# A recurrent attention followed by a SoLU block: first loads split and spread over two queues, one gate block turned on TensorE, one output half moved

## The chip, the cores and the metric

The kernel runs on one core of a Trainium2 chip. The metric is the device time of one execution in microseconds (us), measured without the profiler; the median over the runs counts. One execution was also profiled, and all views below come from that one. TensorE is called PE, VectorE DVE, ScalarE ACT, GpSimd POOL, SyncE SP.

## The reference

Two parts follow each other. The first is a gated linear recurrence over 4 batches, 8 heads, 768 time steps and a head dimension of 48; the second is a feed-forward block on the 3072 tokens, with 384 inputs, 1024 hidden values and 384 outputs.

```python
for t in range(S):
    state = alpha[:, :, t, :, None] * state + np.einsum('bhd,bhe->bhde', k[:, :, t], v[:, :, t])
    y[:, :, t] = np.einsum('bhd,bhde->bhe', q[:, :, t], state)
x = np.ascontiguousarray(y.transpose(0, 2, 1, 3)).reshape(B * S, H * D)
h = x @ w_in
e = np.exp(h - np.max(h, axis=-1, keepdims=True))
solu = h * e / (np.sum(e, axis=-1, keepdims=True) + 1e-09)
mu, var = mean and variance of solu over its last axis
out = ((solu - mu) / np.sqrt(var + 1e-06) * g_ln) @ w_out
```

Inputs q, k, v and alpha are float32. The two weight matrices arrive as float64, so the kernel reads them as pairs of 32-bit words and makes float32 of them itself.

## The kernel before, in words

**Tiling.** Time is cut into 6 groups of 128 steps; one group holds all 4 batches, so it is 512 tokens. Channels are handled transposed (channels on partitions, time along the free axis): the first 32 channels of a head form one block, the last 16 of two heads together another, 12 blocks in all in the tiles `aT` (alpha), `kT`, `qv`, `qe` and `hT`. Products of alpha over time come from scans on DVE: `scan_back` runs backwards over a third of the blocks into `hT`, `scan_on` forwards in `aT`. Keys are multiplied by the one, queries by the other; then `scores` (PE), `masked` (DVE), `read_state` and `read_values` (PE) give the attention output `x`, and `next_state` carries the state on.

**Turning.** The inputs of group 0, and k and q of group 1, are loaded with time on partitions (`load_first`) and turned on PE: `turned` multiplies 48 slices of 32 channels by the identity. The last 16 channels of the heads are first gathered by ACT into a contiguous tile (`ends_of`). All others, alpha of group 1 among them, are loaded in another layout (`load`) and turned by DVE's 32x32 transposes (`alpha_T`, lines L184 and L187). `alpha_over` is a range check of alpha: two passes on ACT over the loaded tile `an` (L201), which must run before the next alpha overwrites it.

**Weights.** Each matrix comes in four pieces of two blocks each, `fetch(i, slot, n)` loading n pieces beginning at piece i. A w_in piece takes 16 DMA issues, 8 of 32 rows and 8 of 16 rows (L505). `in_range` checks a piece on ACT (L522, L523), `bits` makes float32 in five DVE operations (L535 to L547), and `scaled` multiplies a w_out piece by the gain on ACT (L554).

**Feed-forward.** For a group g, `up(g, f)` makes hidden block f of 8: three matmuls into `h` (L366), exponential on ACT (L380), product with h on DVE (L381), square on ACT (L382). `down(n, half)` multiplies four of the eight blocks of one batch-and-group chunk n by w_out into a PSUM tile (L448); after both halves `finish(n)` applies the norm (DVE L457 to L466, POOL L470, ACT L472) and stores.

**Order.** The order on every engine is the order in which the program writes its instructions; each engine runs its own in that order. DMA issues take their turn in the queue of SP (nearly all) or ACT (constants). A start section handles the attention of group 0. Then a loop over f makes the hidden blocks of group 0, with `bits`, `in_range`, loads and `ends_of` for group 1 put between them by hand. Then comes a section, also by hand, that mixes the downs of group 0 with the attention of group 1:

```python
    bits(6)
    tk = three("tp_k", [(ps_a, "a2"), (ps_a, "a3"), (ps_h, "h")])
    turned(kn, ends_k, tk)
    load(k, kn, 2)
    array_sums(0, 1)
    down(0, 0)
    scaled(6)
    bits(7)
    token_sums(0)
    alpha_T(1)
    down(1, 0)
```

It ends with `read_values(1)`, `next_state(1)` and `finish(3)`. From there a loop over g = 1..6 and steps s = 0..7 runs `up(g, s)`, the attention of group g + 1 by a plan, and one half down of group g - 1 at each step, taken from the list `todo`, which is empty for g = 1.

Of the kernel before, what the change touches and what calls it, by code (L numbers as in the profile page):

```python
# [11 lines left out]
U32 = mybir.dt.uint32  # L12
# [4 lines left out]
P = 128  # L17
# [15 lines left out]
def fast_path(ctx, tc, q, k, v, alpha, moe_w_in, moe_w_out, moe_g_ln, out):  # L33
# [12 lines left out]
    nc = tc.nc  # L46
    B, H, S, D = q.shape
# [81 lines left out]
    def load(src, dst, g):  # L129
        t = slice(g * P, (g + 1) * P)  # L130
        for b in range(B):
            nc.sync.dma_start(
                out=dst[32 * b : 32 * b + 32].rearrange("t h u d -> t h (u d)"),
                in_=src[b, :, t, :].rearrange("h (t u) d -> t h (u d)", u=TQ),
            )
# [5 lines left out]
    def load_first(src, dst, g):  # L141
        t = slice(g * P, (g + 1) * P)
        for b in range(0, B, 2):
            nc.sync.dma_start(  # L144
                out=by_token(dst)[:, b : b + 2].rearrange("p b h d -> p (b h) d"),
                in_=src[b : b + 2, :, t].rearrange("b h p d -> p (b h) d"),
            )

    def ends_of(src, tag=None):

        ends = ring.tile([P, T4], FP, name=tag) if tag else two.tile([P, T4], FP, tag="two", name="ends")
        ends = ends.rearrange("p (b d) -> p b d", b=B)
        nc.scalar.copy(out=ends.rearrange("p b (h d) -> p b h d", h=H), in_=by_token(src)[:, :, :, E0:D])
        return ends

    def turned(src, ends, out, blocks=range(NB)):

        x = by_token(src)
        for j in blocks:
            for b in range(B):  # L160
                cols = x[:, b, j, 0:E0] if j < H else ends[:, b, E0 * (j - H) : E0 * (j - H) + E0]
                nc.tensor.matmul(
                    out[j // NP][32 * b : 32 * b + 32, j % NP], lhsT=cols, rhs=ident, start=True, stop=True,
                    tile_position=(0, 32 * b), skip_group_check=True,
                )
# [31 lines left out]
    def alpha_over(g):  # L197
        x = an.rearrange("p h u d -> p (h u d)")
        sq = one.tile([P, 768], FP, name="sq").bitcast(U8)[:, 0 : x.shape[1]]
        for i, sign in enumerate((1.0, -1.0)):  # L200
            nc.scalar.activation(  # L201
                out=sq, in_=x, func=AF.Relu, scale=sign, bias=mone, accum_out=over[:, g, i : i + 1]
            )
# [31 lines left out]
    def apart():  # L235
        for i in range(2):
            nc.scalar.mul(
                out=qv[:, H : 2 * H].rearrange("p (j i) t -> p j i t", i=2)[:, :, i], in_=qe, mul=parity[:, i : i + 1]
            )
# [22 lines left out]
    def scores(g, half, a=None):  # L262
        a = a or banks("a", [NP, P])
        for i in range(NP):
            h = half * NP + i
            for kb, qb in ((h, h), (H + h // 2, H + h)):
                for b in range(B):
                    nc.tensor.matmul(  # L268
                        a[b][:, i], lhsT=kT[quarter(b), kb], rhs=qv[quarter(b), qb], start=kb == h, stop=kb != h,
                        tile_position=(32 * b, 0), skip_group_check=True,  # L270
                    )
        masks[half] = a
# [141 lines left out]
    def warm(n, ps=ps_o, tag="o"):  # L414
        t = ps.tile([P, 512], FP, tag=tag, name="warm")
        for i in range(n):
            nc.tensor.matmul(t[:, 0:P], lhsT=ones, rhs=ones, start=True, stop=True)
# [71 lines left out]

    raws = {}  # L490

    def fetch(i, slot, n=1):

        kind, f = pieces[i]
        w = n * F // (2 if kind else KC)
        raw = room[:, 1536 * slot : 1536 * (slot + n)].bitcast(U32).rearrange("p (c f w) -> p c f w", f=w, w=2)
        if kind:
            parts = [(slice(0, P), c, moe_w_out[(f + c) * P : (f + c + 1) * P, :]) for c in range(2)]
        else:
            rows = moe_w_in[:, f * P : f * P + w].rearrange("(h d) f -> h d f", d=D)  # L500
            parts = [(slice(E0 * r, E0 * r + E0), c, rows[NP * c + r, 0:E0]) for c in range(2) for r in range(NP)]
            parts += [(slice(E1 * h, E1 * h + E1), 2, rows[h, E0:D]) for h in range(H)]
        for rows, c, src in parts:
            if float64:
                nc.sync.dma_start(out=raw[rows, c].rearrange("p f w -> p (f w)"), in_=src.bitcast(U32))  # L505
            else:
                dst = w_out[rows, f + c, 0:DM] if kind else w_in[rows, c, f * P : f * P + w]
                nc.sync.dma_start(out=dst, in_=src)
        for m in range(n):
            raws[i + m] = raw[:, :, w // n * m : w // n * (m + 1)]  # L510

# [37 lines left out]
    def scaled(i):  # L549

        f = pieces[i][1]
        for c in range(f, f + 2):
            w = w_out[:, c, 0:DM]
            nc.scalar.mul(out=w, in_=w, mul=g_col[:, c : c + 1])  # L554
# [27 lines left out]
    def inline(x, name):  # L582
        return nc.inline_tensor(np.ascontiguousarray(x, np.float32), name=name).ap()

    load_first(alpha, an, 0)
    nc.scalar.dma_start(out=ident, in_=inline(np.eye(P), "ident_c"))
    nc.scalar.dma_start(out=mask, in_=inline(np.triu(np.ones((P, P))), "mask_c"))
    odd = np.arange(P) // E1 % 2
# [10 lines left out]
        nc.gpsimd.memset(s, 0.0)  # L599
    nc.gpsimd.memset(state, 0.0)  # L600
    load_v_first(0)
    fetch(0, 3, 2)
    fetch(2, 1, 2)
    nc.vector.memset(ones, 1.0)
    nc.vector.memset(small_ones, 1.0 / 32)
# [5 lines left out]
        return [pool.tile([P, NP, P], FP, tag=tag, name=f"{name}{i}") for i, (pool, tag) in enumerate(where)]  # L611


    warm(18)
    t = three("tp_a", [(ps_a, "a0"), (ps_a, "a1"), (ps_a, "a2")])
    turned(an, ends_of(an), t)
    for i in range(3):
        nc.scalar.copy(out=aT[:, NP * i : NP * i + NP, 1:SW], in_=t[i])  # L618
        scan_back(0, i)
    t = three("tp_k", [(ps_a, "a3"), (ps_h, "h"), (ps_h, "h")])  # L620
    turned(kn, ends_of(kn), t)
    alpha_over(0)
    scan_on(0, 2)
    for i in range(3):
        part = slice(NP * i, NP * i + NP)
# [1 line left out]
    scan_on(0, 0)  # L627
    t = three("tp_q", [(ps_o, "o"), (ps_o, "o"), (ps_a, "a0")])
    turned(qn, ends_of(qn), t)
    for i in (2, 0, 1):  # L630
        if i == 1:
            scan_on(0, i)
        part = slice(NP * i, NP * i + NP)
        nc.vector.tensor_tensor(
            out=qe if i == 2 else qv[:, part], in0=t[i], in1=aT[:, part, 1:SW], op=ALU.mult
        )
        if i == 2:
            apart()
    scores(0, 0)
    t = [x.tile([P, NP, P], FP, tag=n, name="a_" + n) for x, n in ((ps_h, "h"), (ps_o, "o")) for _ in range(2)]  # L640
    scores(0, 1, t)
# [11 lines left out]
    for f in range(FC):  # L653
        p = 2 + f // 2
        up_mm(0, f)
        if f == 4:
            array_sums(0, 0)
        up_act(0, f)
        bits(p, f % 2)
        if f == 0:  # L660
            next_state(0)
            fetch(4, 3)
            load_first(k, kn, 1)
            load_first(q, qn, 1)
            load(alpha, an, 1)
        elif f == 1:
            in_range(2)
        elif f == 2:
            ends_k = ends_of(kn, "e")
        elif f == 3:  # L670
            in_range(3)
            ends_q = ends_of(qn, "u2")
        elif f == 4:
            fetch(5, 1)
            fetch(6, 2)
        elif f == 5:
            in_range(4)
            fetch(7, 3)
            load_v(1)
        elif f == 6:  # L680
            scaled(4)
        elif f == 7:
            scaled(5)
    bits(6)
    tk = three("tp_k", [(ps_a, "a2"), (ps_a, "a3"), (ps_h, "h")])
    turned(kn, ends_k, tk)
    load(k, kn, 2)
# [2 lines left out]
    scaled(6)  # L690
    bits(7)
    token_sums(0)
    alpha_T(1)
    down(1, 0)
    scaled(7)
    tq = three("tp_q", [(ps_a, "a0"), (ps_a, "a1")])
# [37 lines left out]
    read_begin()  # L734
    read_state(0)
    read_state(1)
    down(3, 1)
    read_state(2)
    read_state(3)
    alpha_over(2)  # L740
# [2 lines left out]
        scan_back(2, i)  # L743
    read_values(1)
    next_state(1)
    finish(3)

# [67 lines left out]
            next_state(a)  # L817

    centres = {4: (0, 1), 6: (2, 3), 7: (4, 5, 6, 7)}
    todo = []  # L820
    for g in range(1, G + 1):
        rise, att = g < G, g + 1 < G
        plan = {1: first, 2: second}.get(g, usual)

        def at(where, s):
            for what in plan[where].get(s, "").split() if att else ():
                attend(g + 1, what)

        after = None
        for s in range(FC):  # L830
            at("head", s)
            if rise:
                up(g, s)
            if after is not None:
                finish(after)
                after = None
            if s == 0 and g > 1:
                token_sums(g - 1)
            at("behind", s)
            for f in centres.get(s, ()) if g == 1 else ():  # L840
                centre(f)
            if rise and s:
                running(g, s)
            at("middle", s)
            if todo:
                n, half = todo.pop(0)
                down(n, half)
                if half:
                    after = n
            at("tail", s)  # L850
        if after is not None:
            finish(after)
        todo = [(n, half) for n in range(g * B, g * B + B) for half in range(2)]
# [476 lines left out]
```

## Time and profile before

| | before |
|---|---|
| median of 3 runs (lowest to highest) | 408.06 us (406.02 to 409.49) |
| the profiled execution: its own time | 412.59 us |
| its span from first to last instruction | 409.5 us |
| mean granted PE clock | 0.981 |
| busy: PE, DVE, ACT, POOL | 378.3, 249.8, 146.8, 118.2 us |
| moved by DMA | 30.82 MB |

PE is busy for 92% of the span. Busy shares are averages over stages with different limits, so they have to be read stage by stage: PE is idle for 31 us in all, and all but a few of these lie in the first 165 us and behind the last matmul. A matmul in float32 shows as two records in the trace.

### The profile page before, as it was taken

What the parts mean: (1) busy time and instruction counts of PE and PEld (TensorE: products, weight loads), DVE (VectorE), ACT (ScalarE), POOL (GpSimd) and SP (SyncE); (2) the same over time, 40 slices, a digit from 0 to 9 for tenths busy, and PEclk for the clock granted to TensorE, in tenths of its full rate; (3) what the DMA queues carried; (4) which work ended last, traced back from release to release, by engine and by line L of the source; (5) the groups of instructions that cost most, each with busy time, mean ns of one, the idle gap of its engine ahead of it and who ended that gap; (6) DMA issues with size and microseconds to landing.
All of it is one profiled execution on the core that took longest, in us unless ns stands there. A gap on an engine that the chain in (4) does not pass through costs nothing.

```text
span 409.5 us, 11054 instructions
## 1 busy us (share of the span) xinstructions
PE 378.3 (92%) x4897; PEld 229.9 (56%) x4897; DVE 249.8 (61%) x412; ACT 146.8 (36%) x253; POOL 118.2 (29%) x121
## 2 busy tenths in 40 slices
PE   8786999888997798999999999999999999999991
PEld 8673435456663457555657555666556575554550
DVE  1968789994939884698691894665864322322201
ACT  3533675653332625223443143342251222222110
POOL 4010000030005794075620446210474211333110
PEclk9996999998999999999999999999999999999997
DMA  9966969403329303633030931004200000000110
GB/s 189 183 159 175 216 189 195 106 19 76 81 64 151 78 3 82 78 98 75 23 99 11 162 76 47 9 15 73 26 19 21 22 3 21 19 21 19 40 38 29
DMA packets 86409, 30.82 MB, mean 75 GB/s; under 512 B 67912, under 2 KB 84560, under 8 KB 86352
## 3 DMA queue, kind: packets, MB, share of 16 engines
q1 hardware_dynamic: 85904, 29.89, 33.6%
q8 instruction: 40, 0.66, 0.7%
q10 hardware_dynamic: 448, 0.14, 0.1%
q14 instruction: 17, 0.14, 0.1%
HBM read 25.30 MB, written 4.72 MB: 73 GB/s over the span
## 4 chain that ended last, share of the span: by engine, by line
PE 61%; DVE 21%; SPq 6%; ACT 5%; issue 4%; DMA 2%; DVEq 0%; ACTq 0%
PE o L448 23%; PE h L366 20%; PE y L300 9%; PE a L268 4%; SPq L505 3%; PE kv L342 3%; DVE room L381 3%; DVE aT L209 2%; SPq L144 2%; DVE sT L279 2%; DVE p L392 2%; DVE top L538 1%; DVE aT L184 1%; DMA qn<-in_q_dram 1%; DVE low L546 1%
## 5 line engine op out<-in xcount | busy, mean ns | idle before, releaser
L366 PE MATMUL h<-x,w_in 128*128 128x512 f32 x288 | 135.0, 610 | 8.1 <-DVE g_col L559 4.6
L448 PE MATMUL o<-w_out,room 128*128 128x385 f32 x384 | 133.0, 491 | 1.1 <-DVE least L223 1.1
L448 PEld LDWEIGHTS o<-w_out,room 128*128 128x128 f32 x384 | 71.6, 190 | 57.2 <-issue 15.2
L366 PEld LDWEIGHTS h<-x,w_in 128*128 128x128 f32 x288 | 53.5, 193 | 68.5 <-issue 50.7
L470 POOL TENSOR_TENSOR r<-sums,mhalf 128x1 f32<-128x1 f32 x24 | 13.2, 549 | 192.2 <-DVE sums L462 192.1
L381 DVE TENSOR_TENSOR room<-h,e 128x512 f32<-128x512 f32 x40 | 27.5, 687 | 58.9 <-ACT e L380 58.8
L380 ACT ACTIVATE e<-h 128x512 f32<-128x512 f32 x40 | 23.9, 596 | 83.3 <-PE h L366 83.3
L392 POOL TENSOR_TENSOR p<-p,e 128x512 f32<-128x512 f32 x30 | 42.5, 1417 | 22.7 <-ACT e L380 22.5
L382 ACT ACTIVATE u<-room 128x512 f32<-128x512 f32 x40 | 25.2, 630 | 50.3 <-DVE room L381 50.3
L279 DVE TENSOR_TENSOR sT<-a,mask 128x512 f32<-128x512 f32 x44 | 27.3, 680 | 12.3 <-PE a L268 12.3
L268 PE MATMUL a<-qv,kT 32*128 32x128 f32 x704 | 26.3, 292 | 5.0 <-DVE qv L721 2.0
L268 PEld LDWEIGHTS a<-qv,kT 32*128 32x128 f32 x704 | 23.4, 198 | 12.1 <-issue 2.9
L392 DVE TENSOR_TENSOR p<-p,u 128x512 f32<-128x512 f32 x30 | 23.9, 797 | 9.8 <-ACT u L382 9.8
L209 DVE TENSOR_TENSOR_SCAN hT<-aT,unit 128x516 f32<-128x516 f32 x18 | 21.8, 1256 | 8.2 <-ACT aT L618 8.1
L472 ACT ACTIVATE o_sb<-o,r 128x384 f32<-128x384 f32 x20 | 11.6, 580 | 40.2 <-POOL r L470 37.0
L209 DVE TENSOR_TENSOR_SCAN aT<-aT,seed 128x516 f32<-128x516 f32 x18 | 25.0, 1387 | 0.6
L300 PE MATMUL y<-sT,vn 128*32 128x128 f32 x768 | 23.0, 274 | 1.2 <-issue 0.7
L351 DVE TENSOR_TENSOR state<-state,kv 128x512 f32<-128x512 f32 x10 | 6.9, 688 | 28.2 <-PE kv L342 28.2
L233 POOL TENSOR_TENSOR kT<-kT,hT 128x1024 f32<-128x1024 f32 (+1 forms) x8 | 13.7, 1736 | 31.8 <-DVE kT L184 31.8
L300 PEld LDWEIGHTS y<-sT,vn 128*32 128x32 f32 x768 | 20.8, 110 | 3.6 <-issue 2.6
L331 ACT COPY x<-y 128x384 f32<-128x384 f32 x24 | 11.5, 479 | 31.6 <-PE y L300 31.6
L300 PE MATMUL y<-qv,state 32*32 32x128 f32 x1280 | 20.2, 278 | 2.0 <-issue 1.6
(129 smaller groups left out, 385.4 us busy)
## 6 DMA issues: line engine op xcount, KB each, us to landing
out_dram<-o_sb SPq DMA_DIRECT2D x24, 192.0 KB, 1.9
an<-in_alpha_dram SPq DMA_DIRECT2D x20, 192.0 KB, 4.1
room<-in_moe_w_out_dram SPq DMA_DIRECT2D x8, 384.0 KB, 3.8
kn<-in_k_dram SPq DMA_DIRECT2D x16, 192.0 KB, 4.2
qn<-in_q_dram SPq DMA_DIRECT2D x16, 192.0 KB, 3.5
vn<-in_v_dram SPq DMA_DIRECT2D x5, 512.0 KB, 5.7
room<-in_moe_w_in_dram SPq DMA_DIRECT2D x16, 128.0 KB, 3.6
kn<-in_k_dram SPq DMA_DIRECT2D x4, 384.0 KB, 5.8
```

The lines of the kernel that those rows point to most:

```text
L209: nc.vector.tensor_tensor_scan(out=o, data0=a, data1=s, initial=1.0, op0=ALU.mult, op1=ALU.add)
L233: nc.gpsimd.tensor_tensor(out=kT[:, part], in0=kT[:, part], in1=hk[:, part], op=ALU.mult)
L268: nc.tensor.matmul(a[b][:, i], lhsT=kT[quarter(b), kb], rhs=qv[quarter(b), qb], start=kb == h, stop=kb != h, tile_position=(32 * b, 0), sk ...
L279: nc.vector.tensor_tensor(out=sT[:, b, half * NP : half * NP + NP], in0=a[b], in1=mask[:, None, :].to_broadcast([P, NP, P]), op=ALU.mult,)
L300: nc.tensor.matmul(y_bank(b)[quarter(r), a], lhsT=lhsT, rhs=rhs, start=(b, r) not in begun, stop=stop, tile_position=(row, 32 * r), skip_g ...
L366: nc.tensor.matmul(h, lhsT=w_in[:, a, f * P : (f + 1) * P], rhs=d["x"][:, a].rearrange("p b t -> p (b t)"), start=(a == 0), stop=(a == KC ...
L380: nc.scalar.activation(out=e, in_=h, func=AF.Exp)
L381: nc.vector.tensor_tensor(out=u, in0=h, in1=e, op=ALU.mult)
L382: nc.scalar.activation(out=u2, in_=u, func=AF.Square)
L392: eng.tensor_tensor(out=p, in0=d[0][i] if f == 1 else p, in1=d[f][i], op=ALU.add)
L448: nc.tensor.matmul(d["o"][:, 0 : DM + 1], lhsT=u_of(g, f)[:, b * P : b * P + P], rhs=w_out[:, f], start=(f == 0), stop=(f == FC - 1), skip ...
L470: nc.gpsimd.tensor_tensor(out=r, in0=s[:, 3:4], in1=mhalf, op=ALU.pow)
```

## The change

- Alpha of group 0 is fetched by `load_halves` in eight issues (first four heads of each batch, then the other four) instead of two, and turned in two steps: heads first, each third copied out by ACT as soon as it is there, the gathered ends last. A copy of one column is put first on ACT. The warm-up matmuls go from 18 to 11.
- w_in piece 0 is fetched alone. Piece 1 is fetched by the ACT queue, in three portions of 4, 5 and 7 issues between ACT's work of the start section. `fetch` gets arguments for the queue and for the portion.
- `alpha_over(0)` moves from the start section to f = 2 of the loop over group 0's hidden blocks. The load of group 1's alpha goes behind it, now with time on partitions.
- Group 1's alpha is turned on PE ahead of group 1's k, with `ends_of` at f = 6 and three ACT copies; `alpha_T(1)` goes.
- `down(3, 1)` and `finish(3)` move from the hand-written section into the loop: the half down to step 1 of g = 1, its finish to step 2.

```diff
+    def load_halves(src, dst, g):
+        t = slice(g * P, (g + 1) * P)
+        for h in range(0, H, NP):
+            for b in range(B):
+                nc.sync.dma_start(
+                    out=by_token(dst)[:, b, h : h + NP], in_=src[b, h : h + NP, t].rearrange("h p d -> p h d")
+                )
...
-    def fetch(i, slot, n=1):
+    def fetch(i, slot, n=1, queue=nc.sync, some=slice(None)):
...
-        for rows, c, src in parts:
+        for rows, c, src in parts[some]:
             if float64:
-                nc.sync.dma_start(out=raw[rows, c].rearrange("p f w -> p (f w)"), in_=src.bitcast(U32))
+                queue.dma_start(out=raw[rows, c].rearrange("p f w -> p (f w)"), in_=src.bitcast(U32))
...
-    load_first(alpha, an, 0)
+    load_halves(alpha, an, 0)
...
-    fetch(0, 3, 2)
+    fetch(0, 3)
     fetch(2, 1, 2)
...
-    warm(18)
+    nc.scalar.copy(out=mean_sb[:, 0:1], in_=ones[:, 0:1])
+    warm(11)
     t = three("tp_a", [(ps_a, "a0"), (ps_a, "a1"), (ps_a, "a2")])
-    turned(an, ends_of(an), t)
+
+    def evict_a(i):
+        nc.scalar.copy(out=aT[:, NP * i : NP * i + NP, 1:SW], in_=t[i])
+
+    turned(an, None, t, range(H))
+    evict_a(0)
+    ends = ends_of(an)
+    evict_a(1)
+    turned(an, ends, t, range(H, NB))
+    evict_a(2)
     for i in range(3):
-        nc.scalar.copy(out=aT[:, NP * i : NP * i + NP, 1:SW], in_=t[i])
         scan_back(0, i)
     t = three("tp_k", [(ps_a, "a3"), (ps_h, "h"), (ps_h, "h")])
     turned(kn, ends_of(kn), t)
-    alpha_over(0)
+    fetch(1, 4, queue=nc.scalar, some=slice(0, 4))
     scan_on(0, 2)
...
     turned(qn, ends_of(qn), t)
+    fetch(1, 4, queue=nc.scalar, some=slice(4, 9))
     for i in (2, 0, 1):
...
         if i == 2:
             apart()
+    fetch(1, 4, queue=nc.scalar, some=slice(9, 16))
     scores(0, 0)
...
             load_first(q, qn, 1)
-            load(alpha, an, 1)
         elif f == 1:
             in_range(2)
         elif f == 2:
+            alpha_over(0)
+            load_first(alpha, an, 1)
             ends_k = ends_of(kn, "e")
...
         elif f == 6:
             scaled(4)
+            ends_a = ends_of(an, "e")
         elif f == 7:
             scaled(5)
     bits(6)
+    t = three("tp_a1", [(ps_a, "a2"), (ps_a, "a3"), (ps_o, "o")])
+    nc.gpsimd.memset(aT[:, :, 0:1], 0.0)
+    turned(an, ends_a, t)
+    for i in range(3):
+        evict_a(i)
     tk = three("tp_k", [(ps_a, "a2"), (ps_a, "a3"), (ps_h, "h")])
     turned(kn, ends_k, tk)
...
     token_sums(0)
-    alpha_T(1)
     down(1, 0)
...
     read_state(1)
-    down(3, 1)
     read_state(2)
...
     next_state(1)
-    finish(3)
...
-    todo = []
+    todo = [None, (3, 1)]
...
-            if todo:
-                n, half = todo.pop(0)
+            step = todo.pop(0) if todo else None
+            if step:
+                n, half = step
                 down(n, half)
                 if half:
                     after = n
```

## The prediction, made before the changed kernel ran

> **What bounds the kernel now.** I read the table of busy time by stretch first, to find where TensorE (PE) is not the bound. Columns: start:end, length, then busy us and instructions of PE, PE weight loads, VectorE (DVE), ScalarE (ACT), GpSimd (POOL); the granted PE clock; DMA share; GB/s.
>
> ```profile
> 0.00:20.00 20.00, 16.04 (x352) 14.77 (x356) 10.68 (x23) 9.27 (x13) 5.11 (x12) 1.00 1.04 183
> 20.00:40.00 20.00, 14.69 (x303) 10.25 (x303) 14.87 (x21) 7.86 (x16) 1.83 (x3) 0.83 0.63 162
> 60.00:80.00 20.00, 19.02 (x253) 10.66 (x251) 18.16 (x25) 11.65 (x23) 0.00 (x0) 1.00 0.80 159
> 80.00:100.00 20.00, 15.68 (x135) 10.52 (x134) 16.56 (x31) 10.14 (x19) 4.22 (x5) 0.91 0.07 21
> 120.00:140.00 20.00, 16.03 (x46) 7.12 (x44) 17.93 (x23) 7.24 (x13) 9.77 (x7) 1.00 0.54 91
> 220.00:260.00 40.00, 40.00 (x346) 23.13 (x336) 26.23 (x46) 12.21 (x21) 17.81 (x16) 1.00 0.38 75
> ```
>
> From about 160 us on PE is never idle; whatever the change gains or loses, it does so before. The first 20 us are DMA (share 1.04); 20 to 95 us is a chain through DVE, fed by ACT. So I read the timeline of that part next (start, length, engine, line; in brackets the idle time before it and its releaser).
>
> ```profile
> 20.25 1.77 POOL L180 COPY vn<-room 128x1024 f32<-128x1024 f32 x2 [14.56 <-DMA room<-in_v_dram]
> 29.39 0.95 DVE L535 TENSOR_SCALAR top<-room 128x768 uint32<-128x768 uint32 x1 [3.24 <-DMA room<-in_moe_w_in_dram]
> 34.06 5.33 PE L366 MATMUL h<-x,w_in 128*128 128x512 f32 x6 [4.55 <-DVE g_col L559]
> 49.20 0.63 ACT L382 ACTIVATE sT<-room 128x512 f32<-128x512 f32 x1 [0.76 <-DVE room L381]
> 50.06 0.96 DVE L538 SCALAR_TENSOR_TENSOR top<-room,top 128x768 uint32<-128x768 uint32 x1
> 50.25 0.59 ACT L380 ACTIVATE sT<-h 128x512 f32<-128x512 f32 x1
> 50.94 0.68 DVE L381 TENSOR_TENSOR room<-h,sT 128x512 f32<-128x512 f32 x1
> 67.22 1.12 ACT L554 ACTIVATE w_out<-w_out,g_col 128x384 f32<-128x384 f32 x2 [1.84 <-DVE w_out L547]
> 86.66 0.69 DVE L713 TENSOR_TENSOR qe<-tp_q,aT 128x512 f32<-128x512 f32 x1
> 93.84 3.62 PE L268 MATMUL a<-qv,kT 32*128 32x128 f32 x62 [2.02 <-DVE qv L721]
> 100.18 2.07 PE L268 MATMUL a<-qv,kT 32*128 32x128 f32 x64
> 106.80 2.86 PE L448 MATMUL o<-w_out,room 128*128 128x385 f32 x8
> 133.02 2.84 PE L366 MATMUL h<-x,w_in 128*128 128x512 f32 x6 [2.68 <-DVE room L381]
> ```
>
> To be seen: v lands at 20.25. DVE waits 3.24 us for the first two w_in blocks, which land together at 29.2. PE idles 4.55 us and comes back slow: the first up takes 5.33 us where one at full clock takes 2.84. At 50.9 the product of block 3 waits for its exponential and its own engine almost equally. At 93.84 sixty-two score matmuls take 3.62 us after a pause, sixty-four later ones 2.07.
>
> **Start.** The chain from here on begins when w_in block 0 has landed, since DVE is ready at 26.15. Alone the block is 0.79 MB instead of 1.57, which looks like a gain. But in the built program each DMA signals one of eight semaphores in turn, and an issue waits until the transfer that used its semaphore last has landed. Read off the waits of the built instructions: before, the eighth w_in issue is the one that waits for v to land; now, with eight alpha issues instead of two and the ACT issues taking their turns, it is the third issue of block 0. The seventh alpha issue also waits for the mask, and k for the parity constant, which (issue at 1.64, 3.3 us to landing) arrives at 4.9; k was issued at 2.62. Alpha's own tail and all behind it slip by up to 2.3 us; I take 1.0, as SP runs ahead of the transfers. Nine of the sixteen block-1 issues, now on ACT, go out before v has landed: 0.56 MB, which at the 183 GB/s of the first row takes 3.0 us of a full DMA stretch. From v's landing the remaining fourteen issues of block 0 follow each other every 0.46 us (SP issued 16 in 7.38 us), the last lands 2.2 us after its issue, and some wait in turn for block-1 issues on ACT that hang on the same semaphores: about 8.8 us in all. With v at its old 20.2 that is 29.0 (−0.2); with 2.3 + 3.0 us more it is 34.3 (+5.1). Since block 1's packets are larger and partly fill holes I take a little under the middle: **+2.0**. The earlier alpha scans, the activation table loaded ahead, and seven fewer warm-up matmuls end before that landing and cost or bring nothing while DVE waits there; without that cover k's and q's delay would show, about 1 us.
>
> [...]
>
> **Overflow check moved.** `alpha_over(0)`, two passes over alpha, sat at 11.0 to 14.4 us on ACT, free time before q came. It now stands after the square of up block 2 (49.20) and before `ends_k` and the exponential of block 3 (50.25). Its twin for group 1 ran from 95.43 to 98.78: 3.35 us. DVE was ready for block 3's product at 51.02, the exponential ended at 50.84, so nearly all of it goes into DVE's chain. Later DVE gaps (before 55.23, 61.14, 64.02) are waits for ACT behind the same chain and move along. **+3.35**; between 0 (if ACT had slack) and 3.35. The alpha load of group 1 behind it on SP is late too, but is needed only some 12 us later; `fetch(5,1)` queued behind that load lands with about 3 us to spare. `ends_a` (0.6 us) goes in before the exponential of block 7, which DVE waits for (0.72 us idle before 64.02): **+0.6** (0 to 0.6).
>
> **Alpha of group 1 turned by PE.** Gone from DVE: transposes from 76.16 to 79.00, 2.84 us. Added on PE: 48 turns, 2.84 us by the k turns of 61.77 to 64.61. Added on ACT: three copies of 0.6. Those copies stand behind `scaled(5)`, which waits for DVE's block 5 until 67.22 and ends at 68.34. The k turns reuse the first two banks, so PE cannot start them before 68.94, where it started them at 61.77. Behind them in PE's queue, with their rows of before: k turns and sums 4.64, down(0,0) 2.79, rows 0.59, down(1,0) 2.79, q turns 1.95, mean 1.63, down(0,1) 2.79, mean 0.91, last q turns 1.08. That ends at 88.11, and the product `qe` at 86.66 needs it: **+1.5**. DVE's scans alone would begin 0.9 us earlier than before, so −0.9 is the lower end. PE idles over 4 us ahead of 68.94, as long as the 4.55 us after which it came back slow; I price the slow time by the scores, 3.62 against 2.07: **+1.6** (0, as after the 2.68 us pause before 133.02, to 2.5, as in 5.33 against 2.84). With PE late, the pause before the scores at 93.84 disappears and they run in 2.07: **−1.55** (0 if a pause stays).
>
> **Down(3,1) moved.** From 97.4 to 118.5 PE is full, so taking out eight matmuls brings up(1,0) forward by **−2.8**. They land behind up(1,1), ahead of the 2.68 us in which PE waits for DVE before 133.02, so they cost little there. `finish(3)` goes with them: its four DVE operations (119.19 to 120.26, then idle time) now stand in DVE's full stretch before `scan_on(2,1)`: **+1.1**.
>
> **Sum.** 2.0 + 3.35 + 0.6 + 1.5 + 1.6 − 1.55 − 2.8 + 1.1 = **+5.8 us**. The profiled execution took 412.59 us (span 409.5 and 3.1 around it), so it would take 418.4, 1.4% more; the median of the runs is 408.06, so I predict **413.8 us**. All lower ends give −4.35 (403.7), all upper ends +11.4 (419.5).
>
> **Rivals.** A, not slower: block 0 is there when DVE is, at 26.2. The 3.24 us gap goes, PE pauses 1.3 us instead of 4.55 and the first up takes 2.84: −5.7 instead of +2.0, in all −1.9, **406.2 us**. It decides once block 0 lands before about 28 us, and with a smaller term elsewhere it is clearly faster. For it: half the bytes, and a DVE that idles there. Against: the issue behind v, and nine foreign issues ahead. B: the check lies in ACT time that nobody waits for, +2.4, **410.5 us**. For it: ACT is busy 11.65 of 20 us in the third row. Against: exponential and product are 0.2 us apart at 50.9. C: v slips by the full amount and PE turns slow for longer: 5.8 + 3.1 + 0.9, **418 us**; for it the share of 1.04, against it that packets of block 1 are long.
>
> **How the numbers follow.** Forecast 0.58 (own range 410.5 to 417.5), A 0.18, B 0.13, C 0.11. About 1% is what a measurement here can tell from no change: below 404.0 or above 412.1. Of A 0.13 is faster and 0.05 within; B is within but for 0.02; of the forecast 0.05 is within. That makes faster 0.13, same 0.21, slower 0.66. The range runs from 404, leaving A's fast part out, to 418.5, leaving out the end of C.
>
> **What would show it.** Right: the first DVE bit operation starts after 30 us; a DVE gap of over 3 us ahead of block 3's product with the two alpha passes on ACT in it; PE waiting for an ACT copy of alpha before the k turns of group 1; one down after up(1,1) and no slow clock at group 1's scores. Wrong: that operation starting before 28 us with PE at full clock in the first up, or block 3's product waiting for something other than ACT.

## The result and the profile after

The changed kernel takes 425.52 us (median of 4 runs, 423.51 to 425.76) against 408.77 us (4 runs, 406.02 to 411.52) beside it: 1.0399 times as long, 95% interval 1.032 to 1.0478. Its profiled execution took 425.73 us with a span of 423.1, against 412.59 and 409.5: 13.6 us more of span. The profiled execution of before was one of its longer ones, so the medians lie 3 us further apart than the spans. All that follows compares traces. Runs of one kernel differ by 2.5 to 5.5 us of span, so what one edit does is read from the distance between two instructions of one trace, not from the ends. Each experiment's ratio is against runs of the kernel before made beside it, leaving out runs more than 1.5% above the fastest of the same kernel. The changed kernel was not run again there, so a median 1 to 3 us under its 425.52 us is not by itself clear of noise.

Table of busy time by stretch of the changed kernel (columns as before):

```profile
60.00:80.00 20.00, 15.09 (x187) 9.23 (x190) 16.62 (x23) 12.06 (x25) 0.00 (x0) 0.85 0.76 175
...
120.00:140.00 20.00, 18.17 (x228) 10.57 (x221) 12.28 (x16) 4.97 (x9) 5.48 (x3) 1.00 0.63 115
220.00:260.00 40.00, 38.67 (x594) 23.37 (x593) 26.48 (x42) 11.46 (x22) 11.64 (x10) 1.00 0.43 86
```

PE lost 4 us of work between 60 and 80 us, and its mean clock there fell from 1.00 to 0.85. From 120 to 140 us it has 2.1 us more than before, which is work that comes later now. The last row is the new thing: between 220 and 260 us, where PE was busy for 40.00 of 40 us, it now idles for 1.3 us. The forecast had no term there.

Timeline of the changed kernel, the lines that answer to those of before:

```profile
22.82 1.92 POOL L188 COPY vn<-room 128x1024 f32<-128x1024 f32 x2 [17.11 <-DMA room<-in_v_dram]
...
33.46 0.56 DVE L543 TENSOR_SCALAR top<-room 128x768 uint32<-128x768 uint32 x1 [4.61 <-DMA room<-in_moe_w_in_dram]
...
53.57 1.56 ACT L209 ACTIVATE sq<-an,mone 128x1536 uint8<-128x1536 f32 x1
...
57.96 0.69 DVE L389 TENSOR_TENSOR room<-h,sT 128x512 f32<-128x512 f32 x1 [3.10 <-ACT sT L388]
...
74.60 1.12 ACT L562 ACTIVATE w_out<-w_out,g_col 128x384 f32<-128x384 f32 x2 [1.82 <-DVE w_out L555]
...
76.25 3.64 PE L170 MATMUL tp_k<-ident,kn 128*32 128x128 f32 x64 [4.21 <-ACT aT L627]
79.66 1.60 PE L170 MATMUL tp_k<-ident,e 128*32 128x128 f32 x32
...
103.39 2.68 PE L276 MATMUL a<-qv,kT 32*128 32x128 f32 x64
```

To be seen: v lands 2.6 us later (22.82 against 20.25) and DVE's first bit operation starts 4.1 us later. The first alpha pass starts on ACT at 53.57; the second, the `ends_k` copy and the exponential of block 3 follow, and DVE idles 3.10 us for that. The k turns wait 4.21 us for the copies behind `scaled(5)` (74.60) and then take 5.01 us (76.25 to 81.26) instead of 2.84. The scores of group 1 are no longer paused.

Along the chain, start times in us:

| instruction | before | after | later by | what came in since the row above |
|---|---|---|---|---|
| first DVE bit operation | 29.39 | 33.46 | 4.07 | the start |
| product of block 2 | 48.48 | 52.31 | 3.83 | |
| product of block 3 | 50.94 | 57.96 | 7.02 | overflow check, +3.2 |
| `qe` of group 1 | 86.66 | 96.83 | 10.17 | `ends_a` and alpha's turns, +3.15 |
| scores(1,1) | 100.18 | 108.79 | 8.61 | warm scores, -1.55 |
| up(1,0) | 118.47 | 126.64 | 8.17 | down(3,1) taken out, only -0.45 |
| up(2,0) | 162.76 | 174.98 | 12.22 | `finish(3)` +0.95, and +3.1 more |
| up(3,0) | 221.62 | 235.67 | 14.05 | +1.8 more |
| end of the span | 409.5 | 423.1 | 13.6 | |

Three rows are not as forecast: the down that brought 0.45 us instead of 2.8, and 4.9 us lost behind up(1,0) beyond what `finish(3)` costs there.

**Where the down's gain went.** The PE timeline from the first y read of group 1 to up(1,0), first of the kernel before:

```profile
104.97 1.90 PE L300 MATMUL y<-qv,state 32*32 32x128 f32 x128
106.80 2.86 PE L448 MATMUL o<-w_out,room 128*128 128x385 f32 x8
109.59 1.93 PE L300 MATMUL y<-qv,state 32*32 32x128 f32 x128
111.45 1.06 PE L300 MATMUL y<-sT,vn 128*32 128x128 f32 x26
113.18 2.93 PE L300 MATMUL y<-sT,vn 128*32 128x128 f32 x99 [0.67 <-issue]
...
116.91 1.63 PE L342 MATMUL kv<-vn,kg 128*32 128x64 f32 x70 [0.35 <-issue]
```

and of the changed one:

```profile
113.58 3.02 PE L308 MATMUL y<-qv,state 32*32 32x128 f32 x209
118.07 0.92 PE L308 MATMUL y<-qv,state 32*32 32x128 f32 x47 [1.47 <-issue]
118.92 2.48 PE L308 MATMUL y<-sT,vn 128*32 128x128 f32 x81
121.80 1.41 PE L308 MATMUL y<-sT,vn 128*32 128x128 f32 x44 [0.40 <-issue]
...
126.07 0.64 PE L350 MATMUL kv<-vn,kg 128*32 128x128 f32 x15 [1.43 <-issue]
```

"issue" means that the profile shows nothing for which PE waited. But count the matmul records between two such gaps: 47 + 81 = 128; the 44 and the 84 of the lines left out make 128 again. (What is counted here are the trace's records of matmuls.) With the weight loads these are 256 PE instructions. The DMA table of the trace lists the queue "q8 instruction" with transfers of 16 KB each, 40 in the kernel before (9794 PE instructions, a little over 38 times 256) and 41 in the changed one: 64 bytes for each of 256 instructions. So PE reads its program in blocks of 128 matmuls, and the gaps stand at the borders: the next block is not there yet. The packets of that queue in the trace show it directly (changed kernel, us):

| transfer starts | ends | PE goes on behind its gap | after the end |
|---|---|---|---|
| 115.48 | 116.67 | 118.07 | 1.4 |
| 119.11 | 120.36 | 121.80 | 1.4 |
| 123.55 | 124.58 | 126.07 | 1.5 |

In the fourteen traces of this document PE has 87 gaps of over 0.25 us marked issue, and behind every one it goes on 1.2 to 1.7 us after such a transfer has ended. Of two gaps at neighbouring borders, the transfer for the second starts 1.0 to 3.4 us after PE has passed the first, and PE passes the second 3.45 us or more after the first. Y reads can eat 128 matmuls in less (1.90 us in the first line of before above) and so overtake the transfers; eight matmuls of a down last 2.86 us and are 16 of a block's 256 instructions. Theory S of the experiments is that down(3,1) cost nothing where it stood, because the fetch of the program caught up behind it, and that all else is a plain sum of the parts. Theory F adds that the gaps in the later stretches move with the place of the borders.

### The profile page after: what moved, and what is told of

It reads as the page before. It is cut to its first block, busy times and chain, and to the rows that moved or that the text cites. A ratio compares the mean times of both kernels' runs of the same rounds, so it can differ in the third digit from the quotient of the medians.

```text
span 423.1 us, 11245 instructions
## 1 busy us (share of the span) xinstructions
PE 382.4 (90%) x4979; PEld 231.2 (55%) x4979; DVE 246.4 (58%) x410; ACT 149.1 (35%) x258; POOL 118.4 (28%) x121
## 4 chain that ended last, share of the span: by engine, by line
PE 62%; DVE 14%; DMA 6%; ACT 6%; issue 5%; SPq 4%; POOL 1%; DVEq 0%; ACTq 0%; POOLq 0%
PE o L456 24%; PE h L374 19%; PE y L308 9%; PE a L276 3%; PE kv L350 3%; DMA room<-in_v_dram 2%; DVE room L389 2%; DVE aT L217 2%; DVE sT L287 2%; SPq L144 2%; DVE p L400 2%; SPq L513 1%; DMA room<-in_moe_w_in_dram 1%; DMA qn<-in_q_dram 1%; PE tp_k L170 1%
## 5 line engine op out<-in xcount | busy, mean ns | idle before, releaser
L276 PE MATMUL a<-qv,kT 32*128 32x128 f32 x704 | 24.7, 279 | 3.0 <-DVE least L231 1.5
L276 PEld LDWEIGHTS a<-qv,kT 32*128 32x128 f32 x704 | 21.9, 186 | 10.0 <-issue 2.8
L359 DVE TENSOR_TENSOR state<-state,kv 128x512 f32<-128x512 f32 x10 | 6.9, 688 | 32.1 <-PE kv L350 32.1
L308 PE MATMUL y<-qv,state 32*32 32x128 f32 x1280 | 20.5, 278 | 3.4 <-issue 3.0
```

The source lines that it names most:

```text
L276: nc.tensor.matmul(a[b][:, i], lhsT=kT[quarter(b), kb], rhs=qv[quarter(b), qb], start=kb == h, stop=kb != h, tile_position=(32 * b, 0), sk ...
L308: nc.tensor.matmul(y_bank(b)[quarter(r), a], lhsT=lhsT, rhs=rhs, start=(b, r) not in begun, stop=stop, tile_position=(row, 32 * r), skip_g ...
```

## The experiments

### One part undone at a time

**Down back in its place** (kernel `u_down`):

```diff
     read_state(1)
+    down(3, 1)
     read_state(2)
...
     next_state(1)
+    finish(3)
...
-    todo = [None, (3, 1)]
+    todo = []
```

> The changed kernel with down(3,1) and finish(3) back between the y reads of group 1. Theory S (sum of parts; the y reads are short matmuls that run out of PE instructions, which come in blocks of 128 matmuls, and the eight long matmuls of a down give the fetch time): the PE gaps marked issue between 113 and 127 us fall from 3.30 us to about 1.0, so up(1,0) starts at 126 to 127.5 although 2.8 us of work stand ahead of it again; finish(3) leaves DVE's full stretch, about -1.0: 424.5 us, -0.5 to -2 against the changed kernel. Rival D (the gaps have nothing to do with the down; moving it did bring its 2.8 us): up(1,0) at 129.4, time 2 us longer than the changed kernel.

Measured: median 425.37 us, ratio 1.0417 (1.0314 to 1.0521), span 421.4. PE timeline from the first read:

```profile
113.96 2.86 PE L456 MATMUL o<-w_out,room 128*128 128x385 f32 x8
...
124.72 0.86 PE L350 MATMUL kv<-vn,kg 128*32 128x128 f32 x23 [1.16 <-issue]
125.51 2.84 PE L374 MATMUL h<-x,w_in 128*128 128x512 f32 x6
```

The gaps fall from 3.30 to 1.16 us. From the first read to up(1,0) it takes 13.38 us with the down and took 13.06 without: 2.8 us of work went in for 0.3. S holds here and D, with 2.8 more, fails. The median is that of the changed kernel, and the 0.5 to 2 us less that S expected can't be seen in it.

**The start as before** (`u_start`): `load_first(alpha, an, 0)`, `fetch(0, 3, 2)`, no block 1 on ACT, `warm(18)`, the alpha copies and scans in their old order.

> The changed kernel with the whole start as before (alpha by batches, blocks 0 and 1 in one fetch on SP, 18 warm-ups, no table load ahead); check, turns and down stay moved. Theory S: the first DVE bit operation comes back from 33.5 to 29.4 and everything behind it by 3.7 to 4.1 us: 421.5 us. Rival L (what follows 36 us is late because the start is late: transfers of group 1 collide, ACT and DVE fall out of step): 8 us or more come back, 417 us or less. A second rival, O (the late start is hidden behind the later waits): under 1.5 us comes back.

Measured: 422.51 us, ratio 1.0303 (1.019 to 1.0416), span 420.0, that is 3.1 less. The first bit operation starts at 28.45, up(0,0) at 33.12 (4.6 earlier than changed), and at scores(1,1) 4.4 us are still there. S holds to within 1 us: of the 4.4, 1.3 are given back later, most of it in the read stretches. L and O fail; a late start is not what makes the rest late.

**The check back in the start** (`u_check`):

```diff
     turned(kn, ends_of(kn), t)
+    alpha_over(0)
...
         elif f == 2:
-            alpha_over(0)
             load_first(alpha, an, 1)
```

> The changed kernel with alpha_over(0) back behind the k turns of the start (the alpha load of group 1 stays where the change put it). Theory S: the product of block 3 starts 3.2 us earlier, at 54.7 instead of 57.96, and all behind it: 422.3 us, -2.5 to -3.5. Theory H (the two passes lie in ACT time that nobody waits for; the DVE gap ahead of block 3 has another cause): the product stays at 57 to 58 and the time within 1 us.

Measured: 422.48 us, ratio 1.034 (1.024 to 1.044), span 417.9. DVE's timeline:

```profile
53.66 0.68 DVE L389 TENSOR_TENSOR room<-h,sT 128x512 f32<-128x512 f32 x1
```

This is the product of block 3, and no idle time stands before it. It follows that of block 2 (51.20) by 2.46 us, as before the change, against 5.65 with the check between: 3.2 us, and H fails. (It is 4.3 us earlier than in the changed kernel; the other 1.1 came from a first up of 4.5 us instead of 5.46.)

**Alpha of group 1 transposed by DVE again** (`u_turn`): no turns of `an` by PE, no `evict_a` and no `ends_a` for group 1, `alpha_T(1)` behind `token_sums(0)`.

> The changed kernel with group 1's alpha transposed by DVE as before: no turns by PE, no three ACT copies, no ends_a. Theory S: k turns start without waiting for ACT (no PE gap of 4.2 us, no half clock there), qe moves from 96.8 to about 93.6 (-0.4 for ends_a, -2.8 for the turns); the scores of group 1 take 3.6 us again instead of 2.7, so 1 us of it is given back: 423.5 us, -1 to -3. Rival (DVE's 2.84 us of transposes are on the same chain, so the trade is even): the time within 0.7 us of the changed kernel.

Measured: 422.88 us, ratio 1.0333 (1.0225 to 1.0441), span 419.6. PE timeline:

```profile
66.94 1.96 PE L170 MATMUL tp_k<-ident,kn 128*32 128x128 f32 x64
```

The k turns wait for nothing and run at full clock; `qe` starts at 92.24, 4.6 us earlier, of which 1.35 was there already at the product of block 6. So turns and `ends_a` cost 3.2 us at `qe`. The pause of 2.02 us ahead of the scores is back, 62 of them take 3.39 us, and at scores(1,1) only 3.0 of the 4.6 us are left. S holds.

### What makes each part so dear

**Alpha's load by batches** (`e_alpha`: `load_first(alpha, an, 0)`, the rest as changed) **and block 1 on SP** (`e_sp`: `fetch(1, 4)` behind `fetch(0, 3)`, no transfers on ACT).

> The changed kernel with block 1 fetched by SP behind block 0 instead of by ACT; all else as changed. Theory Q (the late block 0 comes from the nine block 1 transfers that run ahead of v and from the semaphores they hold): v lands at about 20.8 instead of 22.8, the first DVE bit operation starts at 27 to 29 instead of 33.5, up(0,0) at 32 instead of 37.7; block 1 and block 2 land later and take part of it back, so -2.5 to -4 us at the k turns of group 1 and in the time. Theory P (it comes from alpha by halves, whose eight issues delay k, q, v and block 0 alike): the first bit operation stays at 32 or later, the time within 1 us.

> The changed kernel with alpha loaded in two DMAs by batches as before; block 0 alone and block 1 on ACT as changed. Theory P: the first bit operation comes 2 to 4 us earlier than 33.5. Theory Q: it stays within 1 us of 33.5, or comes at most 1.5 us earlier with k and q; the first scan of alpha goes back from 7.7 to about 9.2 us and nobody waits for it. Time by P -2 to -4, by Q within 1.5.

Measured, `e_alpha`: 422.18 us, ratio 1.0238 (1.0093 to 1.0384). DVE's timeline:

```profile
31.05 0.56 DVE L543 TENSOR_SCALAR top<-room 128x768 uint32<-128x768 uint32 x1 [4.19 <-DMA room<-in_moe_w_in_dram]
```

`e_sp`: 427.06 us, ratio 1.04 (1.0302 to 1.0498):

```profile
29.47 0.56 DVE L543 TENSOR_SCALAR top<-room 128x768 uint32<-128x768 uint32 x1 [2.37 <-DMA room<-in_moe_w_in_dram]
...
37.52 0.56 DVE L543 TENSOR_SCALAR top<-room 128x768 uint32<-128x768 uint32 x1 [3.83 <-DMA room<-in_moe_w_in_dram]
```

Each theory was half right. Take away either and v lands at 20.7 or 20.5 us, within the 19.5 to 20.9 of the six traces with the old start; in the six with both changes it lands at 21.3 to 22.8. The first bit operation starts at 27.8 to 29.4 with the old start and at 32.1 to 33.9 with both changes. Alpha's eight issues put k and q back by about 1 us (11.33 and 15.85 in `e_sp`, 10.51 and 14.77 in the kernel before), and so, it seems, into the block 1 transfers that ACT starts at 11.4 us; that this is how they add up is not shown. Taking block 1 off ACT brings the first bit operation forward by 4.0 us, but then DVE waits 3.83 us for block 1 (37.52) and 2.98 us for block 2 (at 45.3): SP has 48 transfers to issue, and in the kernel before it issued 16 of them in 7.38 us. At the k turns of group 1, 1.4 us are left, and nothing at the end; the -2.5 to -4 expected by Q did not come. Loading alpha by batches keeps its 2.4 us: it is 3.25 us ahead at the k turns and 3.2 at the end of the span. So by these two traces the ACT issues cost nothing on balance, and the split alpha load is what to drop; the ratios of the two kernels and of the changed one overlap.

**PE kept at work ahead of the k turns** (`k_warm`, one run):

```diff
+    t = ps_o.tile([P, 512], FP, tag="o", name="fill")
+    for i in range(4):
+        nc.tensor.matmul(t, lhsT=ones, rhs=unit.rearrange("p j s -> p (j s)")[:, 0:512], start=True, stop=True)
     tk = three("tp_k", [(ps_a, "a2"), (ps_a, "a3"), (ps_h, "h")])
```

> The changed kernel with four matmuls of 128x512 (read by nobody) on PE between the alpha turns and the k turns of group 1, in the 4.21 us in which PE waits for ACT's copies. Theory C (the k turns take 5.0 us there because PE comes back at half clock): k turns start at the same distance from scaled(5), take 2.84 us, and down(0,0) and qe come 2.2 us earlier against them than in the changed kernel (qe 18.4 us behind the k turns instead of 20.6). Rival (the turns are slow because k's transposed reads or ACT are): 5 us again, qe unmoved.

Measured: 420.18 us in one run, span 417.7. PE timeline:

```profile
74.81 1.95 PE L170 MATMUL tp_k<-ident,kn 128*32 128x128 f32 x64 [0.58 <-ACT aT L627]
76.58 1.06 PE L170 MATMUL tp_k<-ident,e 128*32 128x128 f32 x32
```

The turns take 2.83 us, and `qe` follows their start by 18.40 us instead of 20.58, as theory C said to the tenth. The granted clock was halved from 73.95 to 80.78 us in the changed kernel; in `k_warm` the 64 turns of the heads take 1.95 us instead of 3.64, as at full clock in the kernel before (64 in 1.95 us, 7.14 to 9.09). Of the 3.15 us that the turns and `ends_a` cost, 2.2 are the half clock after the wait and not the wait itself.

**The block borders moved** (`e_pad`):

```diff
+    pad = ps_a.tile([P, NP, P], FP, tag="a1", name="pad")
+    for i in range(23):
+        nc.tensor.matmul(
+            pad[quarter(i % 4), 0], lhsT=ident[:, 0:32], rhs=ident, start=True, stop=True,
+            tile_position=(0, 32 * (i % 4)), skip_group_check=True,
+        )
     scan_on(0, 2)
```

> The changed kernel with 23 small matmuls more (32x128, read by nobody) on PE between the k and the q turns of the start, where PE waits 3.15 us for q. They are 46 matmul records; with the 82 that the change adds, PE's instruction blocks of 128 matmuls fall on the same work behind the turns of group 1 as before the change. Theory F (the PE gaps marked issue in the y reads of group 2 depend on where the block borders fall): the gaps of 1.55, 0.64 and 2.22 us between 160 and 175 us become one of about 1.6 as before, and up(2,0) follows up(1,0) by 45.5 us instead of 48.3; the time 2 to 3 us below the changed kernel, 422.5. Rival G (the gaps come from transfers or from the number of short matmuls alone): 48.3 us between the two ups and the time within 1 us.

Measured: 421.42 us, ratio 1.0275 (1.0166 to 1.0383), span 417.1. Work was added at the start, and the kernel is if anything faster than the changed one: the two ratios overlap, but the span of the profiled execution is 6.0 us shorter. Of these, 2.3 are there at up(1,0), where the clock was halved in other places (its mean over the span was 0.977, beside 0.979); 3.8 come between up(1,0) and up(3,0). The reads of group 2 on PE, first in the changed kernel:

```profile
160.81 2.46 PE L308 MATMUL y<-qv,state 32*32 32x128 f32 x171
164.82 1.39 PE L308 MATMUL y<-qv,state 32*32 32x128 f32 x85 [1.55 <-issue]
...
173.65 1.41 PE L350 MATMUL kv<-vn,kg 128*32 128x64 f32 x53 [2.22 <-issue]
```

and with the pad:

```profile
158.54 3.79 PE L308 MATMUL y<-qv,state 32*32 32x128 f32 x253
164.17 0.41 PE L308 MATMUL y<-qv,state 32*32 32x128 f32 x3 [1.84 <-issue]
```

The first gap moves from behind the 171st to behind the 253rd matmul of the stretch; in the kernel before it was the 252nd. One more gap of 0.53 us is left, where the changed kernel had 0.64 and 2.22. The stretch shrinks from 14.17 to 12.29 us and the next one, of group 3, from 15.04 to 13.12 (13.19 before). From up(1,0) to up(3,0) it is 105.3 us instead of 109.0. Up(2,0) follows up(1,0) by 46.5 us, where F expected 45.5 and G 48.3. F holds but for the gap that is left, G fails.

All fourteen traces agree with it. The group 3 stretch took 13.1 to 13.5 us in the six kernels in which the next border, counted on in steps of 128 from the last gap of group 2, lies 0 to 9 matmuls behind its start, and 14.5 to 15.6 in the eight with 23 to 55. In the group 2 stretch it is 10.7 to 12.75 us with the border at the 244th to 253rd matmul and 12.7 to 15.0 with 139 to 171. Borders alone don't give the tenth: 252 stood for 10.67, 11.03, 12.40 and 12.75 us in four kernels. Part of that is when the transfer starts. At one border, in the `kv` matmuls of group 2, seven kernels have gaps of 1.29 to 2.55 us, and the transfer started 1.9 us (gap 1.39) to 3.4 us (gap 2.55) after PE had passed the border before. What makes it start late stays open.

**The down moved alone** (`b_down`, one run: the kernel before with the down edits only).

> The kernel before with down(3,1) and finish(3) moved as the change moves them, and nothing else. Theory F (without the eight long matmuls the reads wait for PE instructions): the stretch from the first y read of group 1 to up(1,0) takes 13.0 us instead of 13.5, with PE gaps of about 3 us in it; the scans of group 2 are 0.9 us later behind finish(3), so the time is 0 to +1 us. Rival D: the stretch takes 10.7 us, and the time falls by 1.7.

Measured: 415.04 us, span 411.8. PE timeline:

```profile
108.22 1.49 PE L300 MATMUL y<-qv,state 32*32 32x128 f32 x94 [1.29 <-issue]
...
111.95 2.71 PE L300 MATMUL y<-sT,vn 128*32 128x128 f32 x91 [1.03 <-issue]
...
116.77 1.52 PE L342 MATMUL kv<-vn,kg 128*32 128x64 f32 x62 [1.56 <-issue]
```

13.63 us to up(1,0) with the down gone, 13.50 with it there: gaps of 3.88 us take the whole 2.8. F holds here. By up(2,0) it has even lost 2.4 us, more than the 0 to 1 expected: 0.95 by `finish(3)` on DVE, and 1.7 in the reads of group 2, where PE fell to half clock for 3.4 us in this execution. D fails; in this one execution the move by itself brought no gain.

### A version that beats both

Two PE pauses of the kernel before come with half clock (0.5 from 32.31 to 39.14 and from 93.75 to 97.16 us): 4.55 us ahead of the first up and 2.02 us ahead of the scores of group 1. `e_warm` fills the first with four wide matmuls read by nobody, placed behind `keys_back(0)` and written as in `k_warm`. `b_fill1` fills it with 64 small ones as in `e_pad`, 128 records, so that the borders stay. `b_best` has 24 small and 2 wide ones there, and 38 small ones between `down(2, 0)` and `scores(1, 0)`, again 128 records in all.

> The kernel before, with four matmuls of 128x512 (read by nobody) on PE behind the key turns of the start, in the 4.55 us in which PE waits for w_in. Theory C (PE's half clock behind that pause is on the chain): the first up takes 2.84 us instead of 5.33, the product of block 0 starts at 37.7 instead of 40.1, and 2 to 2.5 us of it stay to the end: 406 us against 408.5 before. Rival (DVE's bits of block 1 end at 38.5 anyway and block 2's transfer lands at 37.4, so DVE is the bound there): 1.6 us earlier at the product of block 0 and under 1 us in the time.

> The kernel before with 64 small matmuls (32x128, read by nobody; 128 records, so one whole instruction block) on PE in the pause ahead of the first up. Theory C and F together: as with the four wide ones the clock stays up and the product of block 0 comes 2 us earlier, and since the block borders stay on the same work, the gaps in the y reads are those of the kernel before (13.5 us from the first read of group 1 to up(1,0), not 14.4), so all 2 us reach the end: ratio 0.995. If F is wrong about the borders: 1 us at the end, ratio 0.998.

> The kernel before with matmuls read by nobody in two PE pauses: 24 small and 2 wide ones ahead of the first up, 38 small ones ahead of the scores of group 1 (128 records in all). Theory C: 2 us at the first up as with the four wide ones, and 1.5 us at the scores, which take 2.1 us instead of 3.6; the borders of the blocks stay where they were: -3.5 us, ratio 0.991. If the second pause has to stay (the filled matmuls end late or the clock is granted by another rule): -2 us, ratio 0.995.

Measured, against the kernel before: `e_warm` 0.9992 (0.995 to 1.0033), `b_fill1` 1.0014 (0.9974 to 1.0054), `b_best` 0.9958 (0.9921 to 0.9996). PE timeline of `b_best`:

```profile
34.68 2.74 PE L366 MATMUL h<-x,w_in 128*128 128x512 f32 x6
...
91.52 2.36 PE L268 MATMUL a<-qv,kT 32*128 32x128 f32 x64
```

The first up takes 2.74 us instead of 5.33, and the product of block 0 starts 1.8 to 2.0 us earlier in all three; in `b_best` the scores have no pause either, and scores(1,1) starts at 96.60, 3.6 us earlier. At up(1,0) 3.2 us are left, at the end of the span 2.0. What is lost lies in the read stretches again: 12.40 us for that of group 2, though its first border is where it was. `b_best` beats both kernels, the one before only just: by 0.04 to 0.8%, as one of three versions tried. `e_warm` and `b_fill1` can't be told from the kernel before. So theory C is right on the chain and was too hopeful for the end in all three.

## Why the prediction was right or wrong

The direction was right and the marks that it named in the profile are there: the bit operation after 30 us, DVE's gap ahead of block 3 with the two passes in it, PE waiting for an alpha copy ahead of the k turns, full clock at group 1's scores with one down behind up(1,1). The size was wrong: +5.8 us of span forecast, +13.6 measured, and the median lies 7 us above the range.

- **Start, +2.0: mis-sized.** It was 3.8 to 4.1, in the upper half of -0.2 to 5.1. The two delays were listed and then a value under the middle was taken, with the argument that long packets fill holes, which no run here tested. By `e_alpha` and `e_sp` v is late only with both.
- **Overflow check, +3.35: right.** 3.2 by the table, 3.2 by `u_check`.
- **`ends_a` and turns, +0.6 + 1.5 + 1.6 = 3.7: right in sum, by some luck,** 3.15 measured. `k_warm` shows that 2.2 of it is the clock, more than the 1.6 taken and within its bound of 2.5; the other two terms, 2.1 together, came to 0.95.
- **Warm scores, -1.55, and `finish(3)`, +1.1: right,** -1.55 and +0.95.
- **Down(3,1) moved, -2.8: this step failed.** It rested on "From 97.4 to 118.5 PE is full". The trace of before had two gaps marked issue in just that stretch, 0.67 and 0.35 us, and they weren't read. PE was that full there only with the down in place: without it, in `b_down`, the gaps in that stretch came to 3.88 us. It brought 0.45; 2.35 us too much was taken off.
- **No term at all behind 160 us.** "From about 160 us on PE is never idle; whatever the change gains or loses, it does so before": the first half is what the trace of before shows, the second is false. The change adds 82 matmul records ahead of the reads, which shifts the block borders, and that cost 3.1 + 1.8 = 4.9 us in two stretches with no edit in them. `e_pad` gets 3.8 of it back with 46 useless records.

Down and borders together are 7.3 of the 7.8 us by which the sum was short; the 1.9 by which the start was short is largely offset by the smaller terms and by 0.45 us regained behind up(3,0). Rival C had the right sign of its two mishaps, but neither is where the time went. Rivals A and B are refuted: the first by 33.46, the second by `u_check`. The last step, from the profiled execution to the median, took 4.5 us off because before's profiled run was long; the changed kernel's is not (425.73 beside 425.52), which is where the other 3.9 of the 11.7 us by which the median lies above 413.8 come from.

## What to carry to other kernels

A PE that the profile shows as full may be held up by the supply of its own program: before taking a long matmul out from between short ones, look for gaps marked issue, count the matmuls between them, and compare their ends with the transfers of the instruction queue. Here the number was 128 records, and 82 more of them ahead cost 4.9 us in two stretches that nobody had edited. And where a wait makes PE pause, look at the granted clock behind it too: of the 3.15 us that the turns of alpha cost here, 2.2 were the clock.

## What the runs showed of the hardware

- PE's program comes in blocks of 128 matmul records in these traces: 47 + 81 and 44 + 84 between three gaps of the changed kernel, with 256 instructions to a 16 KB transfer of the instruction queue (41 of these for 9958 PE instructions, 40 for 9794 in the kernel before). In dense reads a border cost 0.3 to 2.6 us. Without long matmuls two or three borders in a row cost: 1.47, 0.40 and 1.43 us in the changed kernel, 1.16 us at one border alone in `u_down`, with the down back. That it is the fetch is read from the transfers: at all 87 gaps PE goes on 1.2 to 1.7 us after one has ended (1.23 to 1.50 us at the 11 of the two kernels). No run changed the fetch itself.
- The granted PE clock changed in steps of 3.4 us in these traces: but for the end of the program, the half-rate stretches were 6.83 and 3.41 us long in the kernel before, 6.83 and 6.83 us in the changed one, and 3.4 or 6.8 us in the others. What length of pause brings one on is not shown: behind 2.68 us ahead of an up, six matmuls took 2.84 us in the kernel before, as at full clock, while in `u_down` 3.4 us at half clock followed, and ten matmuls took 6.25 us; 2.02 us ahead of the scores was enough in the kernel before (half clock from 93.75 to 97.16 us).
- Two changes to the loads ahead of v delayed it by more than their sum here: with either alone v came no later than it does in some run with the old start (20.5 and 20.7 us beside 19.5 to 20.9), with both at 21.3 to 22.8 us.
